# Weights decoded by an exclusive or with their range checked by a second reading, and a new order of work, in a sparse attention and feed-forward kernel

## The chip, the cores and the metric

The kernel runs on one core of a Trainium2 chip. The metric is the time of one execution on the device in microseconds (us); lower is better. TensorE (PE) multiplies matrices, VectorE (DVE), ScalarE (ACT) and GpSimd (POOL) do the elementwise work, and SyncE (SP) issues nearly all DMAs.

## The reference

A sparse attention (4 batches, 8 heads, 768 positions, head size 64; a position sees the first `n_global` positions and the last `n_local`, at most 8 and 96 here) is followed by a layer norm with gain `g_ln` and a feed-forward block with a residual:

```python
keep = is_global | is_local
scores = np.where(keep, scale * q @ k.T + bias, -1e9)
a = np.exp(scores - max); a = a / (sum(a) + 1e-9)
x = (a @ v).transpose(0, 2, 1, 3).reshape(B, S, H * D)
xn = (x - mu) / np.sqrt(var + 1e-06) * g_ln
out = x + np.maximum(xn @ w_ch1, 0.0) @ w_ch2
```

`w_ch1` is 512 x 2048 and `w_ch2` 2048 x 512. The kernel gets both as 64-bit floating-point words.

## The kernel before

**Tiles and chunks.** The 3072 rows are 24 tiles of 128. Tiles 0 to 3 are the first of each batch and go a short way through the attention in float32 (`quick`); the other 20 go through `keys`, `values`, `queries` and `tile_` (lines 520 to 736) with every operand split into a high and a low float16 part. `normal` (line 737) divides by the row sum, takes the layer norm's statistics, and leaves xn transposed (`xT`, high and low). Two tiles make a chunk, and there are 12 chunks.

**Feed-forward.** For each chunk `ffn1` (line 821) makes 8 steps `F{c}_{f}`, f = 0, 2, ... 14, each of 24 products 128x256 (`f<-xT,w1h` and `f<-xT,w1l`). The second matrix is applied in one of two ways. Chunks below `EVEN` use `ffn2` (line 919): a step is 12 products 128x512 (`f<-w2h,h`). Later chunks use seven products of sums of blocks, as in Strassen's scheme (`seventh`, line 1009): a step is 21 products 128x256 (`m<-w2h,uh`, `m<-t,uh`). For these, DVE forms the sums of blocks of the hidden values (`mixes`, line 860, tile `R`), ACT or DVE splits off their high part (`uh`), DVE or POOL their low part (`ul`); `sums_of_weights` (line 404, tiles `va`, `t`) forms the sums of the weights once; `combine` (line 954) adds the seven results into the output rows (tile `x`) and stores them.

**Weights.** `weight(n)` (line 336) decodes 16 pieces of 128x1024 words, 8 of w1 and 8 of w2, into high and low float16 parts (`w1h`, `w1l`, `w2h`, `w2l`). The raw words stand in the later places of w2h and w2l or in `st`. A piece is loaded by SP (`wb`), then go `below` on ACT (`wr`, the lower word), `signs` on DVE (`ws`, 16 bit), `sizes` on ACT (`wz`, absolute value, with the row sums in `big` for the range check), `whole` on DVE (`ww`, shift and or), `upper` (`wu`, the cast) and `lower` (`wl`, the rest).

**The flag.** At the end `judge`, `across_rows` (one small product `pf`) and `verdict` reduce the range checks to a flag; if it isn't fine, `general` computes everything again. `pf` stands in PE's queue behind the last step of `ffn1`, with the last products of `seventh` behind it.

**Order.** Nothing is ordered by hand. `Plan` (line 91) is a list scheduler that runs when the program is built: each task has an engine, or a choice of engines, a cost in us, the tasks that it waits for, buffers that it takes, and a rank. It places the task that can begin first, the lower rank first, and the order found is the order of each engine's queue. Where PE would idle in the first 90 us of the plan it inserts products `blank` (128x512, results unused). Until PE's plan reaches `EARLY` the table `FAVOR` weighs the choice of engines, then `LATER`; `LEAD` says how many steps ahead the attention of later tiles is due. Costs and tables therefore decide the order of all the work. The profile puts all instructions on one line, so groups are told apart by their tiles.

## Time and profile before

| | before |
|---|---|
| three runs | 607.88, 608.65, 608.71 us |
| median | 608.65 us |
| span of the profiled execution | 605.5 us |
| busy: PE, DVE, ACT, POOL | 98%, 85%, 67%, 27% of the span |
| granted TensorE clock | full in all 40 slices |

The span runs from the first instruction to the last in one profiled execution; its own total time is not listed, and the median of the runs is 3.15 us above the span. The view by stretches cuts the span at the first step of chunk 0's `ffn1` (38.6 us), the first of chunk 1's (73.4), the last step of `ffn2` by even products (about 262), and the last product (600.7).

### The profile page before, as it was taken

Reading aid. Unit: us, or ns where it says so; the run is one execution under the profiler, and the core shown is the slowest. Engines: PE = TensorE matmul, PEld = TensorE weight load, DVE = VectorE, ACT = ScalarE, POOL = GpSimd, SP = SyncE. Lnnn points to the kernel's source line nnn. Section 1 sums busy time; section 2 is a strip of 40 time slices with the busy share of each in tenths; the row PEclk is TensorE's granted clock in tenths of the full one; section 3 lists DMA queues with packets and bytes.
Section 4 is the critical chain, followed back from the end, with each engine's and each line's share of the span. In section 5 each row is a group of like instructions: output and inputs, shape, how many; then the busy total and the mean of one; then the engine's idle time right before and its main releaser. Section 6 shows DMA issues by size and latency. Waiting matters only on the chain.

```text
span 605.5 us, 15320 instructions
## 1 busy us (share of the span) xinstructions
PE 591.0 (98%) x5929; PEld 489.7 (81%) x5929; DVE 514.9 (85%) x1244; ACT 408.6 (67%) x1004; POOL 160.8 (27%) x128
## 2 busy tenths in 40 slices
PE   8989999999999999999999999999999999999996
PEld 4767896556965985789999999999999999988885
DVE  5999999999999989899789999898898788484654
ACT  5988897965677865787765766889856756333330
POOL 2310121306463228242042122152232031040100
PEclk9999999999999999999999999999999999999999
DMA  8993999976879985977748676868865423110001
...
DMA packets 247307, 88.33 MB, mean 146 GB/s; under 512 B 237376, under 2 KB 237376, under 8 KB 247232
## 3 DMA queue, kind: packets, MB, share of 16 engines
...
q10 hardware_dynamic: 288, 0.00, 0.0%
...
## 4 chain that ended last, share of the span: by engine, by line
PE 62%; DVE 5%; DMA 1%; issue 1%; ACT 0%; DVEq 0%
PE f L204 31%; PE m L204 24%; PE s L204 4%; PE pv L204 3%; DMA out_dram<-x 1%; DVE vn L204 1%; DVE T L204 1%; DVE pn L204 1%; DVE x L204 1%; DMA xT<-xn 0%; DVE w2l L204 0%; DVE R L204 0%; DVE xs L204 0%; DVE qn L204 0%; DVE xn L204 0%
## 5 line engine op out<-in xcount | busy, mean ns | idle before, releaser
L204 PE MATMUL f<-xT,w1h 128*128 128x256 f16 x1536 | 256.3, 273 | 4.7 <-DVE xT L204 2.1
L204 PE MATMUL f<-xT,w1l 128*128 128x256 f16 x768 | 209.3, 273 | 0.0
L204 PEld LDWEIGHTS <-w1h 128*128 128x128 f16 x1536 | 147.5, 98 | 21.9 <-DVE xT L204 2.2
L204 DVE SCALAR_TENSOR_TENSOR R<-f,R 128x128 f32<-128x128 f32 x256 | 68.3, 288 | 35.0 <-ACT R L204 29.6
L204 PEld LDWEIGHTS <-uh 128*128 128x128 f16 x896 | 85.9, 98 | 9.4
L204 PEld LDWEIGHTS <-w1l 128*128 128x128 f16 x768 | 75.1, 98 | 9.2 <-issue 0.5
L204 ACT ACTIVATE T<-T,mn 128x256 f32<-128x256 f32 x160 | 80.1, 501 | 3.2
L204 PE MATMUL f<-w2h,h 128*128 128x512 f16 x256 | 80.4, 379 | 0.4 <-DVE h L204 0.4
L204 ACT ACTIVATE uh<-R 128x896 f16<-128x896 f32 x57 | 54.0, 948 | 38.2 <-DVE R L204 37.9
L204 DVE CUSTOM_DVE_ANT_0 T<-s,mask 128x256 f32<-128x256 f32 (+1 forms) x192 | 68.1, 396 | 10.8 <-PE s L204 10.7
L204 ACT ACTIVATE R<-f 128x512 f32<-128x512 f32 x59 | 35.1, 594 | 61.8 <-PE f L204 60.3
L204 PE MATMUL m<-w2h,uh 128*128 128x256 f16 x256 | 69.8, 273 | 0.0
L204 PE MATMUL m<-w2l,uh 128*128 128x256 f16 x256 | 69.8, 273 | 0.0
L204 PE MATMUL m<-w2h,ul 128*128 128x256 f16 x256 | 69.8, 273 | 0.0
L204 PE MATMUL m<-t,uh 128*128 128x256 f16 x384 | 69.5, 273 | 0.0
L204 PEld LDWEIGHTS <-h 128*128 128x128 f16 x384 | 36.3, 98 | 40.0 <-issue 0.6
L204 POOL TENSOR_TENSOR ul<-R,uh 128x896 f16<-128x896 f32 x17 | 32.4, 1907 | 121.4 <-ACT uh L204 121.4
L204 DVE TENSOR_TENSOR ul<-R,uh 128x896 f16<-128x896 f32 x47 | 54.1, 1151 | 12.1 <-ACT uh L204 11.8
L204 POOL TENSOR_TENSOR pn<-T,pn 128x512 f16<-128x512 f32 x27 | 33.8, 1250 | 114.0 <-ACT pn L204 90.1
L204 PE MATMUL s<-kT,qT 128*128 128x128 f16 (+1 forms) x704 | 55.7, 225 | 2.0 <-ACT T L204 0.9
L204 PE MATMUL m<-t,ul 128*128 128x256 f16 x192 | 52.3, 273 | 0.0
L204 ACT ACTIVATE pn<-T 128x512 f16<-128x512 f32 x78 | 48.7, 624 | 2.2 <-DMA xT<-xn 1.1
...
## 6 DMA issues: line engine op xcount, KB each, us to landing
...
kf<-in_k_dram SPq DMA_DIRECT2D x28, 256.0 KB, 3.9
vf<-in_v_dram SPq DMA_DIRECT2D x28, 256.0 KB, 3.4
qf<-in_q_dram SPq DMA_DIRECT2D x24, 256.0 KB, 3.2
out_dram<-x SPq DMA_DIRECT2D x24, 256.0 KB, 2.4
...
```

The source lines that it names most:

```text
L204: ins = getattr(self.engine, name)(*args, **kw)
```

## The change

- **Decoding.** `signs` may run on ACT (14 of 16 pieces do) as a copy to float16; `sizes` is gone; `whole` uses an exclusive or, and the exponent's offset is taken out by a factor `WORD` in `upper` and `lower`. For w1 the factor is g_ln times WORD per row (`gw`), so the layer norm no longer multiplies by g: each w1 piece takes two operations of 128x512 for `upper` (on DVE or ACT) and two for `lower`. `lower` is on DVE only. Signs in the sums of weights follow.
- **Range check.** After score group 1 of the last tile, SP reads all 16.8 MB of words again in 64 loads of 128x256 words (`again`, tasks `V`), 12 buffers deep; DVE gathers each into `seen` (`J`, 128x256). `judge_words` (`JJ`) follows, and `pf` waits for it.
- **Seven products from chunk 3** (`EVEN` 4 to 3). `mixes` is one operation of 2x128 and two of 128 in place of four of 128.
- **Layer norm.** `centred` subtracts and scales in one `tensor_scalar` after POOL's root; the scaled diagonal for the short tiles is gone.
- **Small moves.** `spread_v` (`vn` 16x1024) goes from a DVE copy to a DMA on SP; the first q is loaded from ACT's queue; the two counts are asked for from two queues; the last chunk ends with products 4, 5, 2, and its last row block is stored in two halves.
- **Order.** Costs, `EARLY`, `LEAD`, `FAVOR`, `LATER` are others; the tables `KINDS`, `SHIFT` and `GIVEN` shift ranks and fix engines of single tasks. Work that may go to POOL goes there less: `pn` 27 to 12 and `ul` 17 to 9 on POOL.

```diff
+WORD = -WS * 2.0 ** -128
...
-EVEN = 4
-EARLY = 150.0
-LEAD = 11
+EVEN = 3
+EARLY = 109.65
+LEAD = 4
-FAVOR = {"ACT": SIDE[0], "POOL": SIDE[1]}
-LATER = {"ACT": WEIGH[0], "POOL": WEIGH[1]}
-EITHER = {"ACT": 0.62, "DVE": 0.7}
+FAVOR = {"ACT": 0.05, "POOL": 0.87}
+LATER = {"ACT": -0.91, "POOL": 0.99}
+EITHER = {"ACT": 0.48, "DVE": 0.6}
...
+    task("asked0", "ACT", 0.47, lambda: asked(0), rank=-60, dma=-3.0)
+    task("asked1", "SP", 0.47, lambda: asked(1), rank=-60, dma=-3.0)
...
-        def signs():
+        def signs(engine):
+            if engine == "ACT":
+                act.activation(out=halves[n][:, :, 1].bitcast(F16), in_=staged[n][1].bitcast(F32), func=AF.Copy, scale=2.0 ** -60)
+                return
             vec.tensor_scalar(out=halves[n][:, :, 1], in0=halves[n][:, :, 3], scalar1=0x8000, scalar2=None, op0=ALU.bitwise_and)
-
-        def sizes():
-            hi = staged[n][1]
-            act.activation(out=hi.bitcast(F32), in_=hi.bitcast(F32), func=AF.Abs, scale=2.0 ** -111, accum_out=big[:, n:n + 1])
...
             lo, hi, _, _ = staged[n]
-            vec.scalar_tensor_tensor(out=hi, in0=hi, scalar=3, in1=lo, op0=ALU.logical_shift_left, op1=ALU.bitwise_or)
+            vec.scalar_tensor_tensor(out=hi, in0=hi, scalar=3, in1=lo, op0=ALU.logical_shift_left, op1=ALU.bitwise_xor)
 
         def upper(engine):
-            if engine == "DVE":
-                vec.tensor_copy(out=dh, in_=staged[n][3])
+            word = staged[n][3]
+            if n < NF // 2:
+                k0 = 2 * (n % 2)
+                if engine == "POOL":
+                    pool.tensor_tensor(out=dh, in0=word, in1=gw[:, k0:k0 + 2].unsqueeze(2).to_broadcast([P, 2, 512]), op=ALU.mult)
+                    return
+                for a in range(2):
+                    g_ = gw[:, k0 + a:k0 + a + 1]
+                    if engine == "DVE":
+                        vec.tensor_scalar(out=dh[:, a], in0=word[:, a], scalar1=g_, scalar2=None, op0=ALU.mult)
+                    else:
+                        act.activation(out=dh[:, a], in_=word[:, a], func=AF.Copy, scale=g_)
+            elif engine == "DVE":
+                vec.tensor_scalar(out=dh, in0=word, scalar1=WORD, scalar2=None, op0=ALU.mult)
             elif engine == "POOL":
-                pool.tensor_tensor(out=dh, in0=staged[n][3], in1=fill.unsqueeze(2).to_broadcast([P, 2, 512]), op=ALU.subtract)
+                pool.tensor_scalar(out=dh, in0=word, scalar1=WORD, scalar2=None, op0=ALU.mult)
             else:
-                act.activation(out=dh, in_=staged[n][3], func=AF.Copy)
-
-        def lower(engine):
-            (pool if engine == "POOL" else vec).tensor_tensor(out=dl, in0=staged[n][3], in1=dh, op=ALU.subtract)
+                act.activation(out=dh, in_=word, func=AF.Copy, scale=WORD)
+
+        def lower():
+            word = staged[n][3]
+            if n < NF // 2:
+                for a in range(2):
+                    k0 = 2 * (n % 2) + a
+                    vec.scalar_tensor_tensor(out=dl[:, a], in0=word[:, a], scalar=gw[:, k0:k0 + 1], in1=dh[:, a], op0=ALU.mult, op1=ALU.subtract)
+            else:
+                vec.scalar_tensor_tensor(out=dl, in0=word, scalar=WORD, in1=dh, op0=ALU.mult, op1=ALU.subtract)
...
+        first = n < NF // 2
+        task(f"wr{n}", "ACT", 1.12, below, [f"wb{n}", "starts"], rank=rank)
+        task(f"ws{n}", {"DVE": 1.12, "ACT": 1.13}, 0, signs, [f"wr{n}"], rank=rank, port=True)
+        task(f"ww{n}", "DVE", 1.14, whole, [f"ws{n}"], rank=rank, port=True)
+        task(f"wu{n}", {"ACT": 1.29 if first else 1.05, "POOL": 1.95, "DVE": 0.8 if first else 0.62}, 0, upper, [f"ww{n}", "gw"] + (["wl1"] if n == 8 else []) + (["wl3"] if n in (8, 9, 10, 11) else []) + (["wl7", "wl8"] if n >= 12 else []), rank=rank, port=True)
+        task(f"wl{n}", "DVE", 1.32 if first else 1.14, lower, [f"wu{n}"], rank=rank, port=True)
...
                 def spread_v():
-                    vec.tensor_copy(out=made["vn", t - 1, i - 1][:GK], in_=made["vn", first, 0][:GK])
-
...
-                task(f"gv{b}_{i}", "DVE", 0.42, spread_v, [f"P{t - 1}_3"], rank=rank - 20, port=True)
+                task(f"gv{b}_{i}", "SP", 0.6, spread_v, [f"P{t - 1}_3"], rank=rank - 20, dma=0.3)
...
         def centred():
             xc = made["xc", t] = p2.tile([P, DM], F32, tag="T", name=f"xs{t}", bufs=3)
-            vec.scalar_tensor_tensor(out=xc, in0=xs[t].rearrange("p h d -> p (h d)"), scalar=mv[:, t, 0:1], in1=gb, op0=ALU.subtract, op1=ALU.mult)
-
+            vec.tensor_scalar(out=xc, in0=xs[t].rearrange("p h d -> p (h d)"), scalar1=mv[:, t, 0:1], scalar2=made["rs", t], op0=ALU.subtract, op1=ALU.mult)
...
         def mixes():
             U = made["U", c, f]
             ps = sums1[c, f].rearrange("p a (t n) -> p t a n", t=2)
-            for to, here, there, op in ((2, ps[:, 1, 0], 0, ALU.subtract), (4, ps[:, 1, 0], 3, ALU.add), (5, ps[:, 0, 0], 4, ALU.subtract), (6, ps[:, 0, 1], 5, ALU.add)):
-                vec.scalar_tensor_tensor(out=U[:, to], in0=here, scalar=0.0, in1=U[:, there], op0=ALU.max, op1=op)
+            vec.scalar_tensor_tensor(out=U[:, 2:5:2], in0=ps[:, 1, 0].unsqueeze(1).to_broadcast([P, 2, P]), scalar=0.0, in1=U[:, 0:4:3], op0=ALU.max, op1=ALU.subtract)
+            for to in (5, 6):
+                vec.scalar_tensor_tensor(out=U[:, to], in0=ps[:, 0, to - 5], scalar=0.0, in1=U[:, to - 1], op0=ALU.max, op1=ALU.subtract)
...
-            parts_ = [(every, (j,)) for j in range(4)] + [((m,), (4, 5, 6)) for m in (1, 6, 7, 4)] + [((1, 6, 7), (7,)), ((4,), (7,))] + [((m,), (4, 5, 6, 7)) for m in (5, 3, 2)]
+            parts_ = [(every, (j,)) for j in range(4)] + [((m,), (4, 5, 6)) for m in (1, 6, 7, 3)] + [((1, 6, 7), (7,)), ((3,), (7,))] + [((m,), (4, 5, 6, 7)) for m in (4, 5, 2)]
...
-        parts_ = {0: (0.7, (2, 3), ()), 1: (1.17, (4, 5), ()), 2: (1.36, (1, 6), (f"Dt{c}",)), 3: (1.2, (7,), (f"D{c}_2",))}
+        parts_ = {0: (0.6, (2, 3), ()), 1: (0.93, (4, 5), ()), 2: (1.23, (1, 6), (f"Dt{c}",)), 3: (1.06, (7,), (f"D{c}_2",))}
...
+            parts_.update({1: (0.6, (4, 5), ()), 4: (0.34, (3,), ()), 5: (0.34, (2,), ()), 6: (0.34, (5,), (f"D{c}_1",))})
...
+        task(f"Oh{t0}", "SP", 0.4, lambda: store(t0, hi), [f"D{c}_2", f"D{c}_4", f"D{c}_6"], rank=rank, dma=0.5)
+        task(f"O{t0}", "SP", 0.4, lambda: store(t0, lo), [f"D{c}_2", f"D{c}_5"], rank=rank, dma=0.5)
...
+    def read_again(n, tag):
+        st = again[n] = p2.tile([P, 256], I64, tag=tag, name=f"again{n}", bufs=p2_bufs[tag])
+        if n < 2 * NF:
+            src = w1[n // 8 * P:(n // 8 + 1) * P, n % 8 * 256:(n % 8 + 1) * 256]
+        else:
+            m = n - 2 * NF
+            src = w2[m // 2 * P:(m // 2 + 1) * P, m % 2 * 256:(m % 2 + 1) * 256]
+        load.dma_start(out=st, in_=src)
+
+    def range_of(n):
+        hi = again[n].bitcast(I32).rearrange("p (n two) -> p n two", two=2)[:, :, 1]
+        if n == 0:
+            made["seen"] = p2.tile([P, 256], I32, tag="pT", name="seen", bufs=3)
+            vec.tensor_scalar(out=made["seen"], in0=hi, scalar1=0x30000000, scalar2=None, op0=ALU.bitwise_xor)
+        else:
+            vec.scalar_tensor_tensor(out=made["seen"], in0=hi, scalar=0x30000000, in1=made["seen"], op0=ALU.bitwise_xor, op1=ALU.bitwise_or)
+
+    p2_bufs = {"ld": 6, "kT": 3, "vn": 3}
+    for n_ in range(4 * NF):
+        tag = ("ld", "kT", "ld", "vn")[n_ % 4]
+        task(f"V{n_}", "SP", 0.6, lambda n_=n_, tag=tag: read_again(n_, tag), [f"S{B * NT - 1}_1"], rank=1e4 + n_, take={tag: [f"J{n_}"]}, dma=0.8)
+        task(f"J{n_}", "DVE", 0.33, lambda n_=n_: range_of(n_), [f"V{n_}"] + ([f"J{n_ - 1}"] if n_ else []), rank=1e4 + n_, take={} if n_ else {"pT": ["never"]}, port=True)
 
     def across_rows():
...
-    task("K1", "PE", 0.1, across_rows, ["K0", f"F{NC - 1}_{NF - 2}"], rank=-1e3, take={"s": ["K2"]})
+    task("K0", "DVE", 2.0, judge, [f"M{n_}" for n_ in range(50)] + [f"A{t}" for t in range(B * NT)], rank=1e4)
+    task("JJ", "DVE", 1.2, judge_words, ["K0", f"J{4 * NF - 1}"], rank=1e4)
+    task("K1", "PE", 0.1, across_rows, ["JJ", f"F{NC - 1}_{NF - 2}"], rank=-1e3, take={"s": ["K2"]})
```

The order on ACT in the head, where the first pieces of w1 are decoded (raw words in `w2h` and `w2l`). Before:

```order
L204 ACTIVATE w2h<-w2h,less 128x1024
L204 ACTIVATE pT_1_339<-tp_1_328 128x512
L204 ACTIVATE w2l<-w2l,less 128x1024 x2
L204 ACTIVATE w2h,big<-w2h 128x1024
L204 ACTIVATE kT_0_383<-tk_373 128x512
L204 ACTIVATE w2l,big<-w2l 128x1024
L204 ACTIVATE qT_399<-tq_388 128x512
L204 ACTIVATE w1h<-w2h 128x2x512
L204 ACTIVATE w2l,big<-w2l 128x1024
```

And now:

```order
L236 ACTIVATE w2h<-w2h,less 128x1024
L236 ACTIVATE w2h<-w2h 128x1024
L236 ACTIVATE kT_0_379<-tk_360 128x512
L236 ACTIVATE qT_384<-tq_368 128x512
L236 ACTIVATE w2l<-w2l,less 128x1024
L236 ACTIVATE xT_308<-tx_386 128x4x128
L236 ACTIVATE w2l<-w2l 128x1024
L236 ACTIVATE w2l<-w2l,less 128x1024
L236 ACTIVATE w2l<-w2l 128x1024
```

The pass after `less` is now `signs`, where it was `sizes` with a step of DVE between; the copies of `pT` out of PSUM have left this place for DVE.

The order on PE where chunk 3's second matrix begins. Before, behind all eight `ffn1` steps of chunk 3:

```order
L204 MATMUL s_1_3252<-kT_3_2774,qT 128x128
L204 LDWEIGHTS h_0_2826
L204 MATMUL f_6_3266<-w2h,h_0_2826 128x512
L204 LDWEIGHTS h_0_2826
L204 MATMUL f_6_3266<-w2l,h_0_2826 128x512
```

And now, behind step `f_3_8`:

```order
L236 MATMUL s_0_2991<-kT_2_2902,qT 128x128
L236 LDWEIGHTS uh_0_2832
L236 MATMUL m_0_3000<-w2h,uh_0_2832 128x256
L236 LDWEIGHTS uh_0_2832
L236 MATMUL m_0_3000<-w2l,uh_0_2832 128x256
L236 LDWEIGHTS ul_0_2936
L236 MATMUL m_0_3000<-w2h,ul_0_2936 128x256
```

The eight steps of 12 products have become eight of 21, and the first of them needs `uh` and `ul` of chunk 3, and three steps of `ffn1` fewer lie ahead of it.

The order on DVE at the end, now (before, only the `R`, `ul` and `fine` rows stand there):

```order
L236 SCALAR_TENSOR_TENSOR seen<-again_9338,seen 128x256
L236 TENSOR_TENSOR ul_12_9439<-R,uh_12_9410 128x896
L236 SCALAR_TENSOR_TENSOR seen<-again_9344,seen 128x256
L236 SCALAR_TENSOR_TENSOR seen<-again_9346,seen 128x256
L236 TENSOR_SCALAR seen<-seen 128x256
L236 TENSOR_REDUCE most<-seen 128x1
L236 TENSOR_SCALAR ok<-most 128x1
L236 TENSOR_REDUCE mask_87<-ok 128x1
L236 SCALAR_TENSOR_TENSOR R<-f_11_14_9413,R 128x2x128
```

The last sums of hidden values (`R` of step `f_11_14`) stand behind the last second reads and their verdict.

## Rows read from the trace of the kernel before

**Rows 1.** The page: busy time, share of the span and instructions of each engine.
```profile
PE 591.0 (98%) x5929; PEld 489.7 (81%) x5929; DVE 514.9 (85%) x1244; ACT 408.6 (67%) x1004; POOL 160.8 (27%) x128
```

**Rows 2.** Stretches: length, busy PE, PEld, DVE, ACT, POOL; clock; DMA; GB/s.
```profile
0.00:38.60 38.60, 32.68 (x201) 21.63 (x201) 29.81 (x97) 30.43 (x86) 11.13 (x15) 1.00 0.89 273
38.60:73.40 34.80, 33.10 (x286) 28.65 (x287) 33.15 (x59) 29.31 (x56) 3.87 (x3) 1.00 0.73 208
73.40:262.00 188.60, 186.53 (x1768) 132.65 (x1766) 179.56 (x368) 139.47 (x354) 69.18 (x55) 1.00 0.89 186
262.00:600.70 338.70, 338.66 (x3679) 306.74 (x3676) 271.64 (x721) 209.39 (x511) 76.63 (x56) 1.00 0.51 103
600.70:605.50 4.80, 0.00 (x0) 0.00 (x0) 0.76 (x2) 0.00 (x0) 0.00 (x0) 0.92 0.30 113
```

**Rows 3.** Waits of PE, 0 to 73.4: us in total, times, longest.
```profile
PE f L204 <- DVE xT L204: 2.1, 2, 1.8
...
PE f L204 <- DVE h L204: 1.4, 2, 1.0
```

**Rows 4.** Stretch 0 to 38.6, tile blank alone: length, busy PE.
```profile
0.00:38.60 38.60, 16.61 (x57) 1.00 0.89 273
```

**Rows 5.** Chain of waits around 222.9 and 263.8: start, us, what.
```profile
222.94 2.59 PE f L204 x12
...
263.81 2.29 PE m L204 x21
```

**Rows 6.** Groups by form: out<-in, shapes, count, busy us, mean ns, idle before.
```profile
L204 DVE TENSOR_SCALAR st<-st 128x1024 uint16<-128x1024 uint16 x10 | 13.5, 1387 | 0.0
L204 DVE SCALAR_TENSOR_TENSOR st<-st 128x1024 int32<-128x1024 int32 x10 | 13.2, 1325 | 0.1
L204 ACT ACTIVATE st<-st 128x1024 f32<-128x1024 f32 x10 | 11.5, 1152 | 0.1
L204 DVE TENSOR_TENSOR w1l<-w2h,w1h 128x1024 f16<-128x1024 f32 x3 | 3.7, 1223 | 0.0
L204 DVE SCALAR_TENSOR_TENSOR xs<-x,mv,gb 128x512 f32<-128x512 f32 x24 | 19.3, 810 | 0.0
L204 DVE TENSOR_SCALAR vn<-vf 128x512 f16<-128x512 f32 x2 | 0.8, 417 | 0.4 <-PE pv L204 0.4
L204 DVE COPY pT<-tp 128x512 f32<-128x512 f32 x1 | 0.7, 684 | 0.0
L204 DVE COPY vn<-vn 16x1024 f16<-16x1024 f16 x16 | 9.6, 597 | 2.8 <-PE pv L204 2.8
L204 DVE SCALAR_TENSOR_TENSOR R<-f,R 128x128 f32<-128x128 f32 x256 | 68.3, 288 | 35.0 <-ACT R L204 29.6 <-DVE flag L204 0.7
```

**Rows 7.** Timeline of DVE near 164: start, us, instruction.
```profile
163.69 0.68 DVE L204 TENSOR_TENSOR pn<-T,pn 128x512 f16<-128x512 f32 x1
164.29 1.64 DVE L204 SCALAR_TENSOR_TENSOR qn<-qf,qn 128x512 f16<-128x512 f32 x1
```

**Rows 8.** Timeline of POOL in the same place.
```profile
163.85 1.53 POOL L204 TENSOR_TENSOR t<-va,t 128x512 f16<-128x512 f32 x1 [3.41 <-ACT t L204]
```

**Rows 9.** Stretches 10 to 20 and 525 to 600, columns as in rows 2.
```profile
10.00:20.00 10.00, 8.73 (x61) 6.04 (x59) 8.62 (x44) 8.85 (x35) 3.70 (x2) 1.00 1.01 331
525.00:600.00 75.00, 75.00 (x689) 67.00 (x688) 45.50 (x119) 22.89 (x32) 8.50 (x5) 1.00 0.06 19
```

**Rows 10.** DMA issues of the page: engine, count, KB each, us to landing.
```profile
kf<-in_k_dram SPq DMA_DIRECT2D x28, 256.0 KB, 3.9
...
out_dram<-x SPq DMA_DIRECT2D x24, 256.0 KB, 2.4
```

**Rows 11.** Timeline of DVE behind the last product: start, us, instruction.
```profile
600.70 0.76 DVE L204 SCALAR_TENSOR_TENSOR x<-m,x 128x256 f32<-128x256 f32 x2 [0.54 <-PE m L204]
```

More of the change, by code (lines that the diff above doesn't have):

```diff
@@ L120, in open_ @@
             for engine in tasks[key][0]:
-                ready[engine][key] = max([self.times[a][1] + (lag if self.on[a] != engine else 0.0) for a in after], default=0.0) + slack
+                ready[engine][key] = max([self.times[a][1] + (lag if self.on[a] != engine else -TAIL.get(engine, 0.0)) for a in after], default=0.0) + slack
         for key in tasks:
@@ L166, in order @@
             engines[engine] = t + cost
-            end = t + cost
+            end = t + cost + TAIL.get(engine, 0.0)
             if dma > 0.0:
@@ L259, in starts @@
         pool.memset(half, -0.5)
-        pool.memset(fill, 0.0)
         made["ones"] = const.tile([P, 1], F32, name="ones")
         pool.memset(made["ones"], 1.0)
-    def beside():
-        made["aside"] = aside = p2.tile([P, 1024], F16, tag="pn", name="aside", bufs=3)
-        made["diag"] = [aside[:, 2 * P * n:2 * P * (n + 1)].bitcast(F32) for n in range(4)]
     def blank():
@@ L275, in warm, with asked @@
         act.activation(out=wm[:, 0:1], in_=ident[:, 0:1], func=AF.Copy)
-    def asked():
-        made["asked"] = counts(const, act, n_global, n_local)
+    def asked(n):
+        src = (n_global, n_local)[n]
+        if "asked" not in made:
+            made["asked"] = const.tile([P, 2, 2], I32, name="nn")
+        (act, sp)[n].dma_start(out=made["asked"][:, n, :], in_=src.bitcast(I32).partition_broadcast(P))
     def count():
@@ L380, in weight @@
         before = {7: ["wl0"], 8: ["wl2"]}.get(n, [])
-        task(f"wb{n}", "SP", 0.6, bring, before, rank=rank - 12, take={} if n in homes else {"st": [f"wl{n}"]}, dma=3.0)
-        task(f"wr{n}", "ACT", 1.24, below, [f"wb{n}", "starts"], rank=rank)
-        task(f"ws{n}", "DVE", 0.7, signs, [f"wr{n}"], rank=rank, port=True)
-        task(f"wz{n}", "ACT", 1.2, sizes, [f"ws{n}"], rank=rank)
-        task(f"ww{n}", "DVE", 1.22, whole, [f"wz{n}"], rank=rank, port=True)
-        task(f"wu{n}", {"ACT": 1.17, "POOL": 1.95, "DVE": 0.75}, 0, upper, [f"ww{n}"] + (["wl1"] if n == 8 else []) + (["wl3"] if n in (8, 9, 10, 11) else []) + (["wl7", "wl8"] if n >= 12 else []), rank=rank, port=True)
@@ L387, in weight @@
-        task(f"wl{n}", {"POOL": 2.2, "DVE": 1.24}, 0, lower, [f"wu{n}"], rank=rank, port=True)
+        task(f"wb{n}", "SP", 0.6, bring, before, rank=rank - 12, slack=0.9, take={} if n in homes else {"st": [f"wl{n}"]}, dma=3.0)
+        first = n < NF // 2
+        task(f"wr{n}", "ACT", 1.12, below, [f"wb{n}", "starts"], rank=rank)
+        task(f"ws{n}", {"DVE": 1.12, "ACT": 1.13}, 0, signs, [f"wr{n}"], rank=rank, port=True)
+        task(f"ww{n}", "DVE", 1.14, whole, [f"ws{n}"], rank=rank, port=True)
@@ L438, in chain_of @@
                 last = [key]
-            task(f"yh{n}_{j}", {"ACT": 0.6, "DVE": 0.45}, 0, lambda engine: high(engine, n), last, rank=rank, take={"h": ["never"]} if n == 4 else {}, port=True)
+            task(f"yh{n}_{j}", {"ACT": 0.53, "DVE": 0.34}, 0, lambda engine: high(engine, n), last, rank=rank, take={"h": ["never"]} if n == 4 else {}, port=True)
             task(f"yl{n}_{j}", cost, 0, lambda engine: low(engine, n), [f"yh{n}_{j}"], rank=rank, port=True)
@@ L813, in normal @@
+            task(f"xh{t}", "ACT", 0.49, turned_high, [f"xt{t}"], rank=rank - 4, take=whole)
+            task(f"xl{t}", "DVE", 0.61, turned_low, [f"xh{t}"], rank=rank - 4)
+        else:
+            task(f"xh{t}", "ACT", 0.53, high, [f"C{t}"], rank=rank - 4, take={"pn": [f"xa{t}"]})
+            task(f"xl{t}", "DVE", 0.61, low, [f"xh{t}"], rank=rank - 4, port=True)
             task(f"xa{t}", "SP", 1.35, across, [f"xl{t}"], rank=rank - 12, take=whole, dma=1.47)
@@ L957, in at @@
         def at(m):
-            k, i = WHERE[m]
+            k, i = where(c, m)
             return ms[c, k][:, i]
@@ L1076, in banded @@
         tile_(t, [QUICK[t]] * 2, [[], []])
-    for c in range(NC):
+    for c in range(EVEN):
         if c < 2:
```

207 lines of the change are left out of this document (110 added, 97 removed), and 4 rows, old and new, of the table SHIFT.

## The prediction, made before the result was known

> **What bounds the kernel now.** I read the page's busy times first. PE is busy 591.0 us of a span of 605.5, 98%; DVE has 85%, ACT 67%, POOL 27% [rows 1]. So a saving on another engine counts only where PE waits for that engine, and the second view, the stretches, shows where that is [rows 2]. The idle time of PE is length less busy: 5.92 us up to 38.6, 1.70 up to 73.4, 2.07 up to 262, 0.04 up to 600.7, and 4.80 behind the last product. From 262 to 600.7 PE never waits, so there only fewer products can bring time. The waits of the first 73.4 us are the third view: what ends them is DVE, with the transposed input xT (2.1 us, 1.8 of it at one place, the first step of chunk 0) and with h (1.4) [rows 3]. The idle time understates the waiting: 57 blanks fill 16.61 us of the first stretch, 0.29 us each [rows 4]. Their number is fixed when the program is built; if the real work comes sooner they don't shrink.
>
> **The change, part by part.** The sum is made against the profiled span of 605.5. The median of the three runs, 608.65, is 3.15 above it, and I carry that difference over unchanged.
>
> *Seven products in chunk 3.* In the chain, an even step is 12 products in 2.59 us and a step of seven products is 21 in 2.29 [rows 5]. Eight steps change: 8 x (2.59 - 2.29) = 2.4. PE is the bound there, so all of it counts: **-2.4**, if the sums are ready (a rival below).
>
> *The head.* In the order, the last DVE operation that chunk 0's first step needs (the second xT) has before it: four 16-bit sign passes fewer, 4 x 1.387 = -5.5; one pass over whole words fewer, -1.3; two centrings as tensor_scalar of 128x512, which I price by the vn row, 2 x (0.81 - 0.42) = -0.8; four more copies out of PSUM at 0.684, +2.7; two low parts of 1.223 become four halves, each between 0.61 and 0.81, 0 to +0.8 [rows 6]. A cast and three masks fewer, one more mask and gw are left out. DVE has 4.1 to 4.9 us less to do in a stretch in which it is busy 29.81 of 38.6 [rows 2]. ACT's absolute-value pass (1.152) is replaced by a sign pass of the same shape, which I price the same; ACT gains little, but a piece now changes engines twice less on its way (the order on ACT: signs straight behind the lower word). DVE is the one PE waits for, and about three quarters of the stretch is DVE work; so I pass on three quarters of 4.5: **-3.4**. The second stretch stays: six more blanks, 6 x 0.29 = 1.7, stand where 1.70 of idle was. Bounds: 0, if the loads of the words set the pace; at the other end all 7.62 of idle gone less seven more blanks, 7.62 - 2.0 = 5.6.
>
> *Chunks 1 to 3, 73.4 to 262.* PE idles 2.07, and DVE is busy 179.56 of 188.6 [rows 2]. Two things pull against each other. Over the whole run POOL gets 35 operations less, of which 15 pn and 8 ul go to DVE. A pn on DVE takes 0.68 [rows 7], a ul of 896 elements by the same rate 0.68 x 896 / 512 = 1.2: 15 x 0.68 + 8 x 1.2 = 20 us more. But where a POOL operation runs, a DVE operation beside it can take 1.64 instead of 0.68 [rows 7, 8], so every POOL operation gone gives back up to 0.96: at most 34 us. Fourteen of 16 sign passes of 1.387 leave DVE over the run, ten of them behind the four counted above, and 16 copies of vn (9.6 us in all) for a DMA [rows 6]; against that, R and ul of chunk 3 come earlier. The balance is slightly in DVE's favour, and I let half of the idle time go: **-1.0**. Bounds -2.1 and +4, the upper one being eight steps that each wait half a microsecond for R.
>
> The Trainium skill (SBUF — State Buffer, "SBUF: two separate sides") says that DVE and GpSimd share a pair of ports under an exclusive lock, where the loser waits for a whole instruction if it reads two operands from SBUF. The slow row (qn, 1.64) has both operands in SBUF and stands beside a POOL operation, so the trace agrees; by this rule the new gathering operations J, whose operands both lie in SBUF, would collide with POOL too. In the last 75 us POOL is busy 8.5 [rows 9], so that changes little.
>
> *The tail.* Behind the last product DVE does two operations of 128x256 in 0.76 us, and then a store of 256 KB goes out [rows 11], landing after 2.4 [rows 10]. Now one such operation is left (0.38) and the last store is half as large. **-0.5**. Bounds 0 (the landing doesn't depend on size) and -0.9.
>
> *The second reads.* 64 loads of 256 KB and 64 operations of 128x256 on DVE. They may begin behind step f_10_0; up to pf PE does 15 steps of 24 products, 15 of 21, and six short attention groups, some 15 x 2.62 + 15 x 2.29 + 2.3 = 76 us (2.62 is 24 x 0.109, the rate of the 21 in 2.29). At 331 GB/s, the rate of the stretch from 10 to 20, where the DMA engines are full [rows 9], 64 x 0.79 = 51 us; in the last 75 us they are busy 6%. A load of this size lands after 3.9 us [rows 10], with 12 buffers one each 0.33. DVE: half of 0.76 each [rows 11], 64 x 0.38 = 24 us; a quarter of the 1.325 of a 1024-word pass would be 0.33 each, 21 us [rows 6]. DVE is idle 75 - 45.5 = 29.5 there [rows 9], and R becomes three operations instead of four, 16 steps x less than 0.288. **0**, covered by PE's products. If the cover fails, DVE stands waiting for a read with the sums R and ul behind it, and PE waits for those.
>
> *The rest.* gv as DMA, the counts from two queues, q from ACT's queue: each within the head or covered, 0.
>
> Sum: -2.4 - 3.4 - 1.0 - 0.5 = -7.3. Span 598.2; time **601.3**. (About 0.2%, 1.2 us, is what a measurement can tell from no change.)
>
> **The rivals.**
>
> 1. *The head gives all it can.* DVE's waits are the only ones in rows 3; if ACT's shorter chain also starts the pieces sooner, 5.6 instead of 3.4, and the middle 2.1: span 605.5 - 2.4 - 5.6 - 2.1 - 0.5 = 594.9, time 598.0. Against it: the DMA engines are 89% busy in that stretch, and more blanks were planned, not fewer.
>
> 2. *The head gives nothing, the middle stays.* The loads set the pace (0.89 of the DMA engines up to 38.6 [rows 2]): -2.4 - 0.5, time 605.8. For it: the same words must come in, in the same order.
>
> 3. *DVE becomes the bound in chunks 2 to 4 (slower).* R and ul for chunk 3 come three steps sooner, and DVE has 9 us of air in 188.6 [rows 2]. If the operations moved from POOL (20 us) aren't paid for by fewer collisions, some 11 us are missing and PE waits for ul before each m: time 601.3 + 11 = 612. It decides from the point at which the collisions given back are under about 11 of the possible 34. Against it: up to 262 DVE is at 95% and PE still waits only 2.07.
>
> 4. *The second reads come late (slower).* They have 76 / 64 = 1.19 us each. At 1.4 us each the last verdict is 13 us late, pf holds up PE's queue, and R of the last step stands behind it: 614. Against it: 0.79 at the rate seen.
> The Trainium skill (DMA: Bandwidth & Descriptors, "Bandwidth") asks for 1 MiB or more per DMA, and its fixed cost of 2.0 us (section "Anatomy of one DMA") would make 2.6 us of each 256 KB one behind another, by estimate 166 us, 90 past the window. What it would do here is to leave DVE waiting at each J; the landing of 3.9 with 12 buffers open speaks against it, since 12 fixed costs run side by side.
>
> 5. *The change doesn't do what it says*: the range check fails, the flag sends all to `general`, and the time is far beyond the range.
>
> **How the numbers follow.** Forecast (599 to 603.5) 0.56; rival 1 0.14; rival 2 0.18; rival 3 0.06; rival 4 0.04; rival 5 and the rest 0.02. (Of rival 4's chance, 0.01 is for the page's rule.) The range holds the forecast and rivals 1 and 2, from 597.0 to 606.5; rivals 3 to 5 are left out. Rival 2 with a little loss in the middle (0.03) and rival 3 where half of it is paid back (0.02) end within 0.2% of 608.65: same 0.05. Faster 0.56 + 0.14 + 0.15 = 0.85, slower 0.04 + 0.04 + 0.02 = 0.10.
>
> **What would show it.** Eight groups of 21 products at 2.29 in chunk 3 in place of eight of 12 at 2.59. The first step of chunk 0 near 35.2 and of chunk 1 near 70.0. PE's idle time from there to chunk 4 near 1. No wait of PE for R, ul or the verdict in the last 76 us, reads landing each 0.8 to 1.2, DVE busy near 67 of the last 75. One operation behind the last product. I am wrong if the first step of chunk 0 stays at 38.6 or falls below 33, if PE waits over 3 us in all for R or ul in chunks 3 and 4, or if pf waits.

## The result, and the profile after

The changed kernel takes 616.28 us (median of four runs, 615.54 to 618.37) where the kernel before takes 608.6: a ratio of 1.0138, 95% interval 1.011 to 1.0167, so it is slower by 1.1 to 1.7%. Forecast were 601.3 and faster. The profiled execution of the changed kernel is its slowest run (618.37, span 616.6); the time went as follows.

The busy times of the page, to compare with [rows 1]: PE is busy 2.5 us longer, and POOL 49 less. PE's surplus isn't more work: the run with short sign passes below (e11) has the same products and shows 587.3.

```profile
PE 593.5 (96%) x5992; PEld 497.1 (81%) x5992; DVE 530.2 (86%) x1292; ACT 420.5 (68%) x992; POOL 111.8 (18%) x93
```

The stretches of the changed kernel, with the columns of [rows 2]. The cuts are the first steps of chunks 0, 1 and 2 (42.1, 81.0, 159.4) and the last product (611.7); 264 is only a cut near the 262 of before. The last even product starts at 246.5 in the kernel before, so 262 isn't the last step of `ffn2`, as was said above, and at 208.0 in the changed one.

```profile
0.00:42.10 42.10, 34.24 (x194) 22.03 (x195) 24.57 (x96) 30.77 (x69) 6.66 (x14) 1.00 0.96 275
42.10:81.00 38.90, 34.87 (x286) 28.20 (x285) 32.73 (x64) 38.71 (x62) 6.64 (x6) 1.00 0.53 146
81.00:159.40 78.40, 73.82 (x605) 47.51 (x604) 71.50 (x133) 53.41 (x111) 19.43 (x15) 0.98 0.97 186
159.40:264.00 104.60, 103.19 (x1086) 84.44 (x1087) 99.09 (x228) 75.92 (x204) 27.83 (x22) 1.00 0.84 155
264.00:611.70 347.70, 347.34 (x3826) 314.91 (x3824) 301.90 (x773) 221.72 (x551) 51.20 (x38) 1.00 0.79 163
611.70:616.60 4.90, 0.00 (x0) 0.00 (x0) 0.42 (x1) 0.00 (x0) 0.00 (x0) 0.85 0.32 110
```

The first stretch grew from 38.6 to 42.1, the second from 34.8 to 38.9, and from chunk 1 to chunk 2 it takes 78.4 instead of 72.2 (in the kernel before chunk 2 begins at 145.65). That is 13.8 us lost by 159.4. Everything behind wins 2.7 back. One profile shows one execution: that of e3 below, which differs from the change only at the end, has 40.8, 38.9 and 77.4 for the first three stretches, so a difference of up to 1.4 us between two profiles says nothing by itself. In the second stretch one number stands out: ScalarE, the fourth of the columns of busy time, is at 38.71 of 38.90. Before it was at 29.31 of 34.80 [rows 2].

PE's waits, above the dots up to 81 and below them behind 81 (us in total, times, longest), to compare with [rows 3]:

```profile
PE tk L236 <- DMA kf<-in_k_dram: 3.7, 1, 3.7
PE f L236 <- DVE h L236: 2.6, 2, 1.8
...
PE s L236 <- DVE kT L236: 2.3, 1, 2.3
PE f L236 <- DMA xT<-xn: 1.5, 1, 1.5
PE s L236 <- DVE R L236: 1.4, 1, 1.4
```

Two things stand out. The first transpose (tk) waits 3.7 us for the first k, which the kernel before had in time. And the groups by form show why ScalarE is full: the sign pass, which had been priced like the pass that it replaced, at 1.152 [rows 6], takes 2.5 us, while passes of the same width beside it (the lower word; the cast) take 1.15 to 1.25:

```profile
L236 ACT ACTIVATE st<-st 128x1024 f16<-128x1024 f32 x8 | 20.2, 2521 | 0.2
L236 ACT ACTIVATE st<-st,less 128x1024 int32<-128x1024 uint32 x10 | 12.4, 1240 | 0.0
L236 ACT ACTIVATE w2h<-w2h 128x1024 f16<-128x1024 f32 x3 | 7.6, 2519 | 0.1
L236 ACT ACTIVATE w2l<-w2l 128x1024 f16<-128x1024 f32 x3 | 7.5, 2501 | 0.0
L236 ACT ACTIVATE w2h<-st 128x1024 f16<-128x1024 f32 x4 | 4.6, 1152 | 0.5 <-DVE st L236 0.5
```

### The profile page after: what moved, and what is told of

Its sections match the earlier page's. It is cut to its first block, busy times and chain, and to the rows that moved or that the text cites. A ratio compares the mean times of both kernels' runs of the same rounds, so it can differ in the third digit from the quotient of the medians.

```text
span 616.6 us, 15639 instructions
## 1 busy us (share of the span) xinstructions
PE 593.5 (96%) x5992; PEld 497.1 (81%) x5992; DVE 530.2 (86%) x1292; ACT 420.5 (68%) x992; POOL 111.8 (18%) x93
## 5 line engine op out<-in xcount | busy, mean ns | idle before, releaser
L236 ACT ACTIVATE uh<-R 128x896 f16<-128x896 f32 x72 | 68.0, 945 | 64.5 <-DVE R L236 64.3
L236 PEld LDWEIGHTS <-uh 128*128 128x128 f16 x1008 | 96.4, 98 | 10.5
L236 DVE SCALAR_TENSOR_TENSOR R<-f,R 128x128 f32<-128x128 f32 (+1 forms) x216 | 72.1, 334 | 12.3 <-ACT R L236 7.3
L236 PE MATMUL m<-w2h,uh 128*128 128x256 f16 x288 | 78.5, 273 | 0.0
L236 PE MATMUL m<-w2l,uh 128*128 128x256 f16 x288 | 78.5, 273 | 0.0
L236 PE MATMUL m<-w2h,ul 128*128 128x256 f16 x288 | 78.5, 273 | 0.0
L236 PE MATMUL m<-t,uh 128*128 128x256 f16 x432 | 78.3, 273 | 0.0
L236 DVE TENSOR_TENSOR ul<-R,uh 128x896 f16<-128x896 f32 x63 | 68.7, 1092 | 4.1 <-ACT uh L236 3.7
L236 POOL TENSOR_TENSOR rs<-rs,half 128x1 f32<-128x1 f32 x24 | 21.2, 882 | 237.8 <-DVE rs L236 237.7
L236 DVE TENSOR_TENSOR pn<-T,pn 128x512 f16<-128x512 f32 x68 | 50.3, 740 | 15.8 <-ACT pn L236 15.3
L236 PE MATMUL f<-w2h,h 128*128 128x512 f16 x192 | 60.9, 384 | 0.9 <-DVE h L236 0.9
L236 PEld LDWEIGHTS <-ul 128*128 128x128 f16 x504 | 49.3, 98 | 5.7
```

The lines of the kernel that those rows point to most:

```text
L236: ins = getattr(self.engine, name)(*args, **kw)
```

## The experiments

Each time is a median, beside the kernel before on the same chip in the same comparison; the ratio has its 95% interval. The plan (and with it the order of all work) is the changed kernel's unless something else is said. The short names e1 to e16 in the headings are those of the runs. "Base L" is the kernel of the second run (e2).

### Sign passes on VectorE (e1)

```diff
-            if engine == "ACT":
+            if engine == "none":
                 act.activation(out=halves[n][:, :, 1].bitcast(F16), ...
```

> The changed kernel with all 16 sign passes on VectorE, as the 16-bit operation of before, each at the place in the order where the plan had put it on ScalarE; nothing else differs. Theory A (the sign pass on ScalarE is the fault: 2.52 us in the trace of the changed kernel where 1.15 was priced, ten of them in the first 80 us, ScalarE busy 35.9 of 36.1 us there): ScalarE loses 14 x 2.52 = 35 us, VectorE gains 14 x 1.39 = 19 us, the first step of chunk 1 comes 3 to 5 us sooner than 80.8, the time is 611 to 613.5. Rival B (the first loads alone set the head): under 1 us, 615.5 to 616.5. Rival C (VectorE has no room for them): slower, 618 or more.

Measured: 619.79, ratio 1.0195 (1.0164 to 1.0227), slower than the change itself. Theory A in this form falls; C's forecast came true. The two stretches of the head in this run:

```profile
0.00:40.70 40.70, 32.70 (x194) 21.67 (x195) 28.37 (x99) 23.76 (x74) 4.84 (x13) 1.00 0.96 280
40.70:83.00 42.30, 35.16 (x285) 27.97 (x284) 41.72 (x72) 24.48 (x47) 10.48 (x6) 1.00 0.49 139
```

The first stretch is 1.4 us shorter, no more than two profiles of one order differ by; the second is 3.4 longer, and there VectorE is now at 41.72 of 42.30 and ScalarE at 24.48. So each engine in turn was full in this stretch when it had all the passes (ScalarE 38.71 of 38.90 in the change).

### First loads as before (e2)

```diff
-        (act, sp)[n].dma_start(out=made["asked"][:, n, :], ...
+        (act, act)[n].dma_start(out=made["asked"][:, n, :], ...
-            ... fetch(raw, (name, t), src, name, b, i, act if aside else None) ...
+            ... fetch(raw, (name, t), src, name, b, i, None) ...
```

> The changed kernel with the first loads issued as before: both counts from ScalarE's queue, the first q from SyncE behind the first k. Theory B (the first k lands at 8.4 us instead of 4.6, since the counts stand ahead of it and q runs beside it): k lands at about 4.7, the first step of chunk 0 moves from 42.1 to about 38.5 to 39.5, and the time falls by 2.5 to 3.7 us, to about 612.5 to 613.8. Theory A alone (ScalarE's sign passes set the head whatever the start): k lands sooner too, but ScalarE's chain takes it back, under 1 us gained, 615.5 or more.

Measured: 612.87, ratio 1.007 (1.0044 to 1.0095). Theory B holds: the first product of k, at 8.44 in the changed kernel, comes at 4.76, chunk 0 begins at 37.7, and chunk 1 at 76.6. The gain is 3.4 us by the medians and 4.1 by the ratios, a little more than forecast. The second stretch is unchanged, 38.9 with ScalarE at 38.71:

```profile
0.00:37.70 37.70, 31.77 (x194) 19.97 (x195) 24.52 (x96) 30.58 (x69) 6.62 (x14) 1.00 0.99 289
37.70:76.60 38.90, 34.87 (x285) 28.18 (x284) 32.76 (x64) 38.71 (x61) 6.63 (x6) 1.00 0.59 164
76.60:155.40 78.80, 74.04 (x606) 47.32 (x604) 71.59 (x133) 53.62 (x111) 19.50 (x15) 0.98 0.91 185
```

PE's timeline at the start, changed kernel first:

```profile
1.58 3.17 PE L236 MATMUL blank<-ident 128*128 128x512 f16 x7 [1.58 <-DVE ident L236]
8.44 1.12 PE L236 MATMUL tk<-ident,kf 128*128 128x128 f32 x4 [3.69 <-DMA kf<-in_k_dram]
```

and with the first loads as before:

```profile
4.76 0.65 PE L236 MATMUL tk<-ident,kf 128*128 128x128 f32 x4 [0.16 <-DMA kf<-in_k_dram]
```

### Both together (e5)

> Both edits together, sign passes on VectorE and first loads as before. If A and B are two causes that add: 608 to 610.5, the first step of chunk 1 at 72 to 74. If they are one queue in two places: not better than the better of the two by over 1 us. If the head was all of the loss: 606 or less, since chunk 3 then gives its 2.4.

Measured: 615.94, ratio 1.013 (1.0102 to 1.0158). Against e1 the loads give 0.65% (3.9 us in one comparison), as they gave 0.68% against the change; the two effects add, with opposite signs. Of the three outcomes named, the first and the third didn't come. The second came by its words (615.94 is not better than the 612.87 of e2), but not for its reason: e1 had made the kernel slower, and the loads gave back what they give alone.

### The two loads apart (e14, e15)

Of the two lines of e2, the first alone (counts) and the second alone (q).

> The changed kernel with both counts from ScalarE's queue; q stays on ScalarE's queue. If the counts ahead of it hold k up: k lands near 5, the first product of it starts at about 5 instead of 8.4, time 612.5 to 613.5. If q beside it holds it up: k lands near 8, under 1 us gained, 615.5 or more.

> The changed kernel with the first q from SyncE's queue; the second count stays ahead of k there. If the counts hold k up: under 1 us gained, 615.5 or more. If q beside it does: 612.5 to 613.5.

Measured: 617.28, ratio 1.0155 (1.0129 to 1.0182), and 614.41, ratio 1.0113 (1.009 to 1.0137). With the counts moved alone, k is there 4.2 us after its issue instead of 7.1, at 5.1, but q, now third in ScalarE's queue, at 9.0, and PE waits for that; chunk 0 begins at 41.4:

```profile
PE tq L236 <- DMA qf<-in_q_dram: 2.0, 1, 2.0
```

With q moved alone, k is there at 6.5 and chunk 0 begins at 39.3. By the ratios 1.5 us are gained, but the interval overlaps with that of the change, so the time alone doesn't show it. So neither expectation is right by itself: the first scores need k and q, and each edit alone leaves one of them late.

The DMA engines show what the count does at the head of SyncE's queue. Between 2.2 and 4.2 us they are 5% busy in the change and 65% in e2 (the last two columns are their share and GB/s); e15 has 20%, e14, with no count in that queue, 53%:

```profile
2.20:4.20 2.00, 2.00 (x6) 0.60 (x4) 0.00 (x0) 1.01 (x2) 0.00 (x0) 1.00 0.05 4
2.20:4.20 2.00, 2.00 (x6) 0.60 (x4) 0.00 (x0) 1.02 (x2) 0.00 (x0) 1.00 0.65 137
```

So behind the count the first k hardly moves before 4.2 us, and with q beside it PE gets it later still (7.1 us after its issue, against 5.2 in e15).

### One second read instead of 64 (e3)

Tasks V and J for the first block alone; the range check of the other words is left out.

> The changed kernel with one second read instead of 64 (the range check of the other 63/64 of the words is left out). Theory (the second reads are covered: in the trace of the changed kernel the engine of products idles 0.36 us from 520 on, 0.3 of it before the product of the verdict): 0.3 to 0.6 us less, 615.7 to 616. Rival (64 loads of 256 KB and 64 operations hold up the end): 5 us or more less, 611 or below.

Measured: 615.63, ratio 1.0124 (1.0096 to 1.0152), where the change has 1.0138: as the theory says, too little to be told apart. The same was asked again of a kernel that doesn't wait elsewhere (e16, below).

### Half of the sign passes on each engine (e10)

```diff
-            if engine == "ACT":
+            if engine == "ACT" and n % 2 == 0:
```

> The changed kernel with the first loads as before (call it base L, 612.9 in the last comparison, where before stood at 607.5) and the sign passes of the odd pieces on VectorE, those of the even pieces on ScalarE, each in its old place. In L ScalarE is busy 38.7 of the 38.9 us between the first steps of chunks 0 and 1; with all passes on VectorE that engine is busy 42.7 of 43.7 and ScalarE 24.4. Theory A' (decoding is bound by the sum of both engines, and one of them is overfull either way): with about half there the stretch falls to 35 to 37 us, and the time by 2 to 4 us against L, to a ratio of about 1.002 to 1.004. Rival (the place in the order is what costs, not the load): between the two, 40 us or more, no gain.

Measured: 611.14, ratio 1.005 (1.0031 to 1.0068), about 1.2 us better than L, though the two intervals overlap. What gain there is lies elsewhere than expected: chunk 0 begins at 35.9 instead of 37.7, and the second stretch is still 38.9, with VectorE at 96% and ScalarE at 87%:

```profile
0.00:35.90 35.90, 32.07 (x195) 20.72 (x196) 25.67 (x97) 27.61 (x75) 4.85 (x13) 1.00 0.98 286
35.90:74.80 38.90, 34.49 (x286) 27.79 (x285) 37.27 (x68) 33.73 (x52) 9.28 (x6) 1.00 0.64 180
```

Neither theory A' (35 to 37) nor its rival (40 or more) came. Both engines have some air here and the stretch is as long as ever, so a full engine isn't all of it. That a pass which is 1.4 us too long also delays what stands behind it, in an order fixed for short passes, is an explanation that this run doesn't show by itself.

### The sign pass in three kinds (e9)

```diff
-act.activation(out=halves[n][:, :, 1].bitcast(F16), ..., scale=2.0 ** -60)
+act.activation(out=halves[n][:, :, 1].bitcast((F16, F16, BF16)[n % 3]), ..., scale=(2.0 ** -60, 0.0, 0.0)[n % 3])
```

> Base L with the sign pass on ScalarE in three kinds, by piece number modulo 3: as it is (float16, factor 2^-60), float16 with factor 0, bfloat16 with factor 0; all leave plus or minus zero. Theory E1 (the product falls below the smallest float16 and that is slow): 2.5, 1.2 and 1.2 us. Theory E2 (writing two bytes at every eighth byte is slow, whatever is written): 2.5 in all three. Theory E3 (the conversion to float16 is slow): 2.5, 2.5 and 1.2.

One run, 614.09 us; the pieces with factor 0 lose their signs, so that part is left out there. Three sign passes in a row are float16 with factor 0, bfloat16 with factor 0, float16 with the old factor; between them stand two passes of `below`, which write four bytes at the same step of eight:

```profile
24.85 2.51 ACT L236 ACTIVATE w2h<-w2h 128x1024 f16<-128x1024 f32 x1
28.16 1.25 ACT L236 ACTIVATE w2l<-w2l,less 128x1024 int32<-128x1024 uint32 x1
29.77 2.49 ACT L236 ACTIVATE w2l<-w2l 128x1024 bf16<-128x1024 f32 x1
32.00 1.20 ACT L236 ACTIVATE w2l<-w2l,less 128x1024 int32<-128x1024 uint32 x1
33.24 2.55 ACT L236 ACTIVATE w2l<-w2l 128x1024 f16<-128x1024 f32 x1
```

E2 holds: neither the small result nor the kind of float matters, all are at 2.5. A float16 result written side by side takes 1.15 (the cast, above) and a four-byte result at every eighth byte 1.2; two bytes at every eighth byte take twice that. Whether a smaller step, or another place within the eight bytes, would be as slow is left open; no run varies them.

### Short sign passes (e11, e16)

```diff
-act.activation(out=halves[n][:, :, 1]..., in_=staged[n][1]..., ...
+act.activation(out=halves[n][:, :448, 1]..., in_=staged[n][1][:, :448]..., ...
```

> Base L with ScalarE's sign passes over 448 of the 1024 words, so that one takes about 1.2 us, near the 1.15 that the plan and the prediction had for it; the signs of the other words are left out. Order of work unchanged. Theory F (the sign pass's price is what upsets the order made for 1.13): the first step of chunk 0 at 36, of chunk 1 at 71 to 72.5 (L: 76.6), the stretch from there to chunk 2 at 73 to 75 (L: 78.8), the time 6 to 9 us under L, a ratio of 0.993 to 0.997. Rival G (the stretch from chunk 1 to chunk 2 is lost to VectorE's and GpSimd's collisions and to the centring behind GpSimd's root, whatever ScalarE does): that stretch stays at 77 to 79, the time 3 to 5 under L, ratio 0.999 to 1.002.

Measured: **601.2**, ratio 0.9883 (0.986 to 0.9906), 1.9% under L. Theory F holds, and the gain is larger than its range. The sign pass takes 1.22 us here:

```profile
L236 ACT ACTIVATE st<-st 128x448 f16<-128x448 f32 x8 | 9.8, 1221 | 0.2
```

The stretches:

```profile
0.00:33.60 33.60, 30.81 (x194) 20.29 (x195) 24.72 (x96) 26.46 (x75) 5.04 (x14) 1.00 0.98 277
33.60:68.20 34.60, 33.88 (x287) 28.09 (x285) 33.73 (x65) 31.10 (x57) 9.11 (x6) 1.00 0.79 230
68.20:142.90 74.70, 72.35 (x607) 46.90 (x605) 71.66 (x133) 48.05 (x109) 19.70 (x14) 1.00 1.00 196
```

Against L (37.7, 38.9, 78.8) all three shrink, by 4.1, 4.3 and 4.1. The third is the telling one: VectorE has the same work there, 71.66 and 71.59 us, and only ScalarE's passes differ. So of the 6.6 us that L loses between chunks 1 and 2 (78.8 against 72.2), 4.1 go with the long passes, and 2.5 remain for everything else, rival G's collisions and the centring behind POOL's root among it.

The collisions are there all the same. In the change PE's longest wait in that stretch, for kT, ends behind three operations of VectorE that run beside POOL (busy almost without a gap from 128.9 to 135.0) and take 1.38, 1.64 and 1.14 us, where the same forms elsewhere take 0.54, 0.69 and 0.19:

```profile
129.96 1.38 DVE L236 TENSOR_SCALAR xs<-x,mv,rs 128x512 f32<-128x512 f32 x1
131.26 1.64 DVE L236 TENSOR_TENSOR pn<-T,pn 128x512 f16<-128x512 f32 x1
132.82 1.14 DVE L236 COPY kT<-kT 128x128 f16<-128x128 f16 x1
134.01 1.01 PE L236 MATMUL s<-kT,qT 128*128 128x128 f16 x8 [2.25 <-DVE kT L236]
```

With short sign passes the same three stand beside the same POOL operations and take as long (1.38, 1.64, 1.14, from 114.6 on), and PE waits 0.3 for kT. So the collision alone doesn't make PE wait there; with the long passes it does. With one second read instead of 64 on top:

> The run with short sign passes (601.2 where before was 608.7, ratio 0.988; the signs of 576 of each 1024 words left out there) with one second read instead of 64 as well (the range check of the other words left out). Forecast's term: the same within 0.6 us, ratio 0.987 to 0.988. Rival (the reads cost, hidden so far behind other waits): 2 us or more less, ratio 0.985 or below.

Measured: 601.01, ratio 0.9893 (0.9874 to 0.9912). The second reads cost nothing that can be told, and the head repeats: chunks 0, 1 and 2 begin at 33.7, 68.1 and 142.9.

### Each sign pass cut in two (e12, e13)

```diff
-act.activation(out=halves[n][:, :, 1]..., ...
+act.activation(out=halves[n][:, :512, 1]..., ...
+vec.tensor_scalar(out=halves[n][:, 512:, 1], in0=halves[n][:, 512:, 3], scalar1=0x8000, ...
```

> Base L, all signs kept: each sign pass that stood on ScalarE is cut in two, 512 words on ScalarE (about 1.36 us by the run with 448 words at 1.22) and 512 on VectorE (about 0.7), in the same place of the order. By theory F the short pass lets the order keep its times, as with the signs left out, less what 14 x 0.6 = 8 us more on VectorE cost where that engine is 95% busy: 603 to 607, a ratio of 0.991 to 0.998, faster than both kernels. Rival (VectorE pays in full, as when it had all 16 passes): 608 to 612.

> The same with 704 words on ScalarE (about 1.8 us) and 320 on VectorE (about 0.45). By theory F with ScalarE's pass as the dearer part: 605 to 609, 1 to 3 us slower than with 512. Rival (VectorE's part is the dearer): faster than with 512.

Measured: 607.16, ratio 0.9994 (0.9983 to 1.0005), and 607.21, ratio 0.9997 (0.998 to 1.0014). Both do all the work, both are as fast as the kernel before, and neither is faster. The truth lies between theory (at most 0.998) and rival (608 or more): 512 words cost ScalarE 1.36 us, and VectorE's half takes about 0.82, 14 of them 11 us, on an engine that is then at 37.72 of 38.3 us between chunks 0 and 1:

```profile
34.90:73.20 38.30, 33.98 (x285) 28.01 (x284) 37.72 (x72) 31.55 (x53) 9.64 (x6) 1.00 0.66 192
L236 ACT ACTIVATE st<-st 128x512 f16<-128x512 f32 x8 | 10.9, 1364 | 0.2
L236 DVE TENSOR_SCALAR st<-st 128x512 uint16<-128x512 uint16 x8 | 6.6, 822 | 0.0
```

With 704 words ScalarE's pass takes 1.79, 0.43 more, and VectorE's about 0.6, 0.2 less, and the time is the same. It lies in the range forecast for the second cut, but neither of the two differences from the first cut came (1 to 3 us slower, or faster), and which of the two engines holds these kernels up isn't shown.

### The sign pass at its true price in the plan (e6)

```diff
-        task(f"ws{n}", {"DVE": 1.12, "ACT": 1.13}, 0, signs, ...
+        task(f"ws{n}", {"DVE": 1.3, "ACT": 2.43}, 0, signs, ...
```

> Base L with the sign pass priced in the plan as the trace shows it, 2.43 on ScalarE and 1.3 on VectorE in place of 1.13 and 1.12, and all the order made anew (9 of 16 passes stay on ScalarE). Theory A' : the stretch between the first steps of chunks 0 and 1 falls from 38.9 to 35 to 37, and PE's waits up to 160 shrink from about 6 to 3 to 4, in all 3 to 6 us less than L, a ratio of 0.999 to 1.002 to before. Rival (the tables of ranks were set for the old prices, so a new order does as much harm as good): within 2 us of L.

Measured: 618.71, ratio 1.0172 (1.015 to 1.0194), 1% slower than L. The stretch between chunks 0 and 1 does fall, to 31.9 us, but chunk 0 begins at 41.5, and chunk 2 comes 85.3 us after chunk 1. What PE waits for there is a transpose that the new order lets come late (7.6 us in one place). The new order also has 103 blanks where L has 78:

```profile
PE f L236 <- DMA xT<-xn: 8.5, 3, 7.6
```

### Even products in chunk 3, and seven products in the kernel before (e7, e8)

`EVEN = 4` in base L; `EVEN = 3` in the kernel before.

> Base L with chunk 3's second matrix by even products, as before, and the order made anew. Theory D (seven products in chunk 3 pull the sums of weights and of hidden values forward, onto VectorE, and cost in chunks 1 to 3 what they save): from the first step of chunk 1 to that of chunk 2 it takes 72 to 75 instead of 78.8 us, the time is within 2 us of L although eight steps take 2.4 more. Rival (seven products there are worth their 2.4): 1.5 to 3.5 us slower than L.

> The kernel before with seven products from chunk 3 alone, its plan's costs unchanged. If the 2.4 are free: a ratio of 0.996 (605 where before is 607.5). By theory D: 0.999 or more, with new waits of PE for VectorE between 73 and 230 of 2 us or more.

Measured: 617.75, ratio 1.0147 (1.0126 to 1.0169), and 628.15, ratio 1.032 (1.0297 to 1.0342). Both are inconclusive on what seven products are worth, since both make the order anew, and both new orders have longer waits than the kernels they came from: in the first a step waits 5.3 us for a sum of weights, in the second the second product of attention waits 6.3 for pT and steps 6.1 for R, the sums of hidden values, 3.9 of it between 160 and 230.

```profile
PE f L236 <- DVE va L236: 5.3, 1, 5.3
```

```profile
PE pv L204 <- DMA pT<-pn: 6.3, 2, 4.7
PE f L204 <- DVE R L204: 6.1, 3, 3.1
```

In the first, chunk 1 to chunk 2 still takes 78.5 us with even products in chunk 3, which speaks against theory D there. The second is as theory D forecast it: a ratio over 0.999, a new wait for VectorE of over 2 us, and from chunk 1 to chunk 2 77.4 us where the kernel before has 72.2. With the order made anew in both, neither settles D; it may have a part in the 2.5 us that e11 leaves. All three kernels whose order was made anew were 4.7 us or more slower than the one they came from. In two of them (e6, e7) the ranks of single tasks had been set for another order (`SHIFT`); the kernel before has no such table and lost most, so the table isn't shown to be the reason.

## Why the prediction was wrong

**The head (forecast -3.4).** Two steps of it failed. One is the sentence that ScalarE's absolute-value pass "is replaced by a sign pass of the same shape, which I price the same": the shape read and the count of words are the same, the layout written is not, and 1.152 became 2.52. Fourteen passes at 1.37 more are 19 us on ScalarE, ten of them in the first 81 us. The range given for the head, 0 to -5.6, had no case in which a pass gets dearer on an engine that PE hardly waits for. Cut short to 1.22, the passes give 11.4 to 11.7 us back (e11 against L). The Trainium skill (ScalarE: Activation LUTs, "Step-by-step: what each stage is for") states one element per cycle and lane, 0.833 ns, whatever the function; the cast of 1.152 is near that by estimate (0.186 us fixed, which the same page states, and 1024 x 0.833 ns make 1.04), the sign pass at 2.52 isn't. The measurement decides: the rule doesn't hold for two-byte results eight bytes apart.

The other is "the counts from two queues, q from ACT's queue: each within the head or covered, 0". The first loads cost 3.4 to 4.1 us (e2 against the change), seen as the first product of k at 8.4 instead of 4.8. Two things hold k up: the count ahead of it, behind which the DMA engines stand nearly idle until 4.2, and the company of q, v and the first megabyte of words, all issued between 1.25 and 2.54. Why a load of 1 KB holds up what is behind it no run shows. For the company, the Trainium skill (DMA: Bandwidth & Descriptors, "Queues, rings and completion order") says that a DMA engine serves its queues in turn, packet by packet; e15 agrees with it in that taking q off the second queue brings k from 8.4 to 6.5, the count still ahead.

With both undone (e11; signs of 576 of 1024 words left out) chunk 0 begins at 33.6 and chunk 1 at 68.2, 5.2 us sooner than in the kernel before: near the far end of the range.

**Chunks 1 to 3 (-1.0).** Wrong in size and sign: +6.2 us up to chunk 2 with the passes at 2.5 (+5.1 in e3's profile), of which the first reason accounts for the larger part, and still +2.5 with short ones. The balance of VectorE and POOL, on which the step rested, was not in VectorE's favour: its work in that stretch is 71.50 against 70.32 before. The centring, priced at 0.42 by the vn row, takes 0.54 in the head and 1.38 in both places of this stretch, beside POOL. What the 2.5 are made of stays open.

There is a second-order loss in it. Behind the wait of 2.25 us for kT, at 134, five products of 512 columns start 0.43 us apart instead of 0.216, half the rate (1.2 instead of 2.4 GHz), and the stretch from 130 to 140 has a mean granted clock of 0.83 (the column behind the busy times):

```profile
134.82 0.63 PE L236 MATMUL f<-w2h,h 128*128 128x512 f16 x1
135.25 0.63 PE L236 MATMUL f<-w2l,h 128*128 128x512 f16 x1
130.00:140.00 10.00, 7.75 (x62) 4.26 (x61) 9.42 (x22) 5.48 (x17) 4.94 (x4) 0.83 0.72 136
```

The five cost 1.05 us more than at the full rate. So a wait of PE can cost more than itself, but doesn't always: in e3 and e15 the same wait (2.3 and 2.2) stands in the same place, the products behind it start 0.216 apart, and the stretch between chunks 1 and 2 takes 77.4, about 1 us less than in the change and L.

**Seven products (-2.4).** Borne out by the counts and durations: the even steps lose 64 products of w2h and 32 of w2l (x192 and x96 left), the others gain 168 at 0.109. No run isolates it, since every change of `EVEN` makes the order anew; what it is worth in time isn't shown.

**The tail (-0.5).** One operation is left behind the last product, as forecast, but the stretch is 4.90 instead of 4.80. The operation takes 0.42 where the two took 0.76 [rows 11], but the cut into halves adds a third store to SyncE's queue, where before there were two: the three issues take 2.06 us instead of 1.63, the last one ends 1.7 us behind the last product, and the smaller store lands after 2.4 us, as the larger did before [rows 10]. SyncE's queue at the end, the changed kernel first, then the one before:

```profile
611.33 2.06 SPq L236 DMA_DIRECT2D out_dram<-x  x3
600.18 1.63 SPq L204 DMA_DIRECT2D out_dram<-x  x2
```

**The second reads (0).** Right. With the 64 reads the rate is 254 GB/s in the 76 us from 526 on, PE is busy 75.85 of 76, and pf waits 0.3:

```profile
526.00:602.00 76.00, 75.85 (x738) 67.97 (x736) 70.39 (x183) 29.90 (x53) 6.90 (x5) 1.00 0.83 254
L236 DVE SCALAR_TENSOR_TENSOR seen<-again,seen 128x256 int32<-128x256 int32 x63 | 26.6, 423 | 3.5 <-DMA again<-in_moe_w_ch_dram 2.1
again<-in_moe_w_ch_dram SPq DMA_DIRECT2D x64, 256.0 KB, 5.3
```

J takes 0.423, over the bounds of 0.33 to 0.38, and fills VectorE to 70.39. Rival 4 is out, and so is the page's rule as it was drawn there: the reads land after 5.3 us each, up to twelve at a time, so one comes every 1.2 us. (The page's fixed cost is measured on DMAs that GpSimd issues; these are issued by SyncE.)

**The rivals.** None named what happened. Rival 2 (loads set the pace) comes nearest for the start, and rival 3 (an engine overfull) has the right form with the wrong engine: it looked at VectorE at 95%, not at ScalarE at 67%. That e11 lands at 601.2, where 601.3 was forecast, is luck: its head gives 5.2 us where 3.4 were forecast, the way from chunk 1 to chunk 2 loses 2.5 where up to 1.0 was to be gained, and everything behind gives 4.0 where 2.9 were forecast. And that kernel leaves signs out; with all of them kept (e12) it is as fast as the kernel before.
